# Loading queries as four tokens a partition and reading them with a stride on TensorE, with later state copies and score pairs

## The chip, the cores and the metric

One core of one Trainium2 chip. The metric is the device time of one execution in microseconds (us). Every time below is a median of several executions, but for three kernels that were run once; "the span" is the length of the one execution that the profiler recorded, some 1 to 2 us shorter. The granted TensorE clock of the kernel before, as a share of full speed, was above 0.99.

## The reference, cut to what matters

Linear attention with decay ("retention"), then a two-layer network with a tanh GELU, on B = 8 batches, H = 8 heads, S = 576 tokens, D = 64:

```python
scores = scale * np.matmul(q, k.transpose(0, 1, 3, 2))
gamma = 1.0 - 2.0 ** (-5.0 - np.arange(H))
Dmat = np.where(rel >= 0, gamma[:, None, None] ** rel, 0.0)      # rel = i - j
attn_out = np.matmul(scores * Dmat, v)
x = attn_out.transpose(0, 2, 1, 3).reshape(B * S, H * D)         # 4608 x 512
h = x @ w_in                                                     # 512 -> 2048
out = gelu_tanh(h) @ w_out                                       # 2048 -> 512
```

## The kernel before: the parts that matter

The 512 first tokens of a batch are four chunks c of 128 tokens, the other 64 are a tail. q and k are loaded as fp32, cast to fp16 with the decay folded in, and transposed, so that the head dimension lies on the partitions (tile `tt`: [128, q or k, 16 blocks, 128 tokens]). Per chunk, TensorE makes the scores `st` from k and q, VectorE masks them, and TensorE makes the values `xs` from them and v and adds what the state of all earlier chunks (`tbd`) gives for q. ScalarE copies `xs` as fp16 to `xT`, the input of the network. Its first layer gives `hp`, which ScalarE turns into `gT` with the gelu. The second layer is seven products of halves, summed in `opA`, `opB` and `opC`; for these VectorE makes sums `s` of parts of `gT` (the profile's lines call the sums `s` or `gT`). `ost` is a tile of the output. `cq` and `ck` are the casts of q and k, `eq` and `ek` those of the tail, `ld` and `lt` what was loaded. Batches 0 and 1 already load q with four consecutive tokens on a partition (1 KB runs); batches 2 to 7 load one token a partition (256 B runs):

```python
def load(b, key, c, u=0):
    ...
    elif key == "q" and b < NQ:                       # NQ = 2
        nc.sync.dma_start(
            out=t.rearrange("p (h x) -> p h x", h=2),
            in_=src[b, 2 * c : 2 * c + 2, 0:M0, :].rearrange("h (p j) d -> p h (j d)", j=QT),   # 1 KB runs
        )
    else:
        nc.sync.dma_start(
            out=t.rearrange("p (h d) -> p h d", d=D),
            in_=src[b, :, 128 * c : 128 * c + 128, :].rearrange("h s d -> s h d"),              # 256 B runs
        )
```

For batches 0 and 1 the permutation of the tokens is undone by the TensorE transposes, which write PSUM with a step of four (`turn_q4`). From batch 3 on the transpose is a DMA (`turn_dma`), which undoes nothing. The reads of q, by scores and by states:

```python
def tq(b, c, p):                                      # the moving operand: 128 tokens
    d, o = turned(b, c)
    return d[:, 1, 4 * p + c if b < NQ and c < NC else o + p, :]
...
# score(), two heads of a pair in the two row groups:
nc.tensor.matmul(st[hl][:, 128 * p : 128 * p + 128], d[r, 0, o + p, :], tq(b, c, p)[r], start=True, stop=True)
...
# inter(), "states" in this text:
nc.tensor.matmul(xs[:, 128 * p : 128 * p + 128], tbd[b % 2][:, c - 1, p, :], tq(b, c, p),
                 start=False, stop=True, skip_group_check=True)
...
# put(): ScalarE brings the values to the network's input
src = xs.rearrange("p (n g t) -> p g n t", n=HP, g=2)
nc.scalar.copy(out=xT[:, g0 : g0 + 2], in_=src)
```

The network of batch t runs interleaved with the attention of batch t + 1. A stage counts TensorE steps u of some 0.86 us, and attention work hangs on them:

```python
def states(t, u, b, c, tag):
    ...
    def sp(n, hl):                                    # ScalarE copies a state into tbd
        at(t, u + 2 + 2 * n + hl, lambda: spread(b, c + n, A.copy, (hl,)))
...
            u0, u1, u2, u3 = (8, 14, 19, 25) if t == 2 else (7, 13, 19, 25) if t == 3 else (6, 12, 19, 25)
            scores(t, u0, (b, 0, ...), (b, 1, ...), *tail)
        states(t, u1, b, 2, "t0")
        values(t, u1, (b, 0, "t1"), (b, 1, "t2"), ...)
        scores(t, u2, (b, 2, ("hp", "hp")), (b, 3, ("t1", "t2")))
```

## Time and profile before

| | before |
|---|---|
| time, median of the first 3 runs | 304.36 us (304.33 to 305.08) |
| span of the profiled execution | 302.8 us |
| busiest engines | TensorE 96%, VectorE 58%, ScalarE 57%, GpSimd 40% |
| fifth matmul of the network to the last matmul, from start to start | 277.1 us |
| last matmul's start to the end of the span | 4.76 us |

The last two rows are read from the trace's records of TensorE. The last but one is called the network stretch below; it begins with the fifth matmul, because the four before it wait in part for the last casts of the weights. Two more are needed here, the groups that the strided read will touch, with shapes kept apart. Columns: line, engine, operation, output<-input, shapes, count | busy us, mean ns of one | idle time before.

```profile
L317 PE MATMUL st<-tt 64*128 64x128 f16 x256 | 10.8, 218 | 1.2 <-DMA tt<-cq 0.5 <-ACT xT L405 0.5
L388 PE MATMUL xs<-tt,tbd 128*128 128x128 f16 x96 | 8.5, 221 | 0.0
```

The mean of 218 ns is not the cost of a matmul: successive matmuls overlap, and the recorded end is modelled. 256 scores are busy for 10.8 us together. The cost is the distance from start to start, which the chain of work that ended last gives in order of time (start, us, engine, what, line, count):

```profile
139.65 0.55 PE st L317 x16
...
146.38 0.55 PE xs L388 x8
```

Sixteen scores, two at a time, are eight steps; eight states are eight steps. From records start to start each is 56 ns, like the contiguous transposes of 128 columns in the same trace.

### The profile page before, as it was taken

How to read it: one execution, taken by the hardware profiler on the slowest of the kernel's cores; microseconds unless marked ns; L12 is line 12 of the kernel's file. 1: busy time of each engine (PE TensorE's matmuls, PEld its weight loads, DVE VectorE, ACT ScalarE, POOL GpSimd, SP SyncE). 2: the span in 40 equal slices, each digit the busy share in tenths (PEclk: the TensorE clock that was granted, in tenths of full speed). 3: DMA queues.
4: the chain of work that ended last, by engine and by line, in shares of the span. 5: the costliest groups of instructions: out<-in, count | busy, mean ns of one | idle time of the engine just before them, and what ended most of it. 6: DMA issues, size and time to landing. Idle time of an engine off the chain costs nothing.

```text
span 302.8 us, 6867 instructions
## 1 busy us (share of the span) xinstructions
PE 291.9 (96%) x2747; PEld 197.4 (65%) x2747; DVE 175.9 (58%) x359; ACT 173.0 (57%) x332; POOL 120.2 (40%) x178
## 2 busy tenths in 40 slices
PE   6899999999999999999999999999999999999994
PEld 2568755788784588458845884578456844784583
DVE  6650879678962866386547653855396435342423
ACT  6676417998657573658366736593647246316620
POOL 8668315550924179106910591049757110000000
PEclk9999999999999999999999999999999999999998
DMA  7999999999999996999599959953962140103004
GB/s 203 216 296 391 387 286 224 203 263 242 201 189 230 201 261 125 221 208 255 100 219 209 239 66 203 225 133 65 276 79 60 32 157 11 26 20 121 2 0 139
DMA packets 130592, 52.87 MB, mean 175 GB/s; under 512 B 118785, under 2 KB 121345, under 8 KB 130561
## 3 DMA queue, kind: packets, MB, share of 16 engines
q1 hardware_dynamic: 128544, 48.77, 74.2%
q0 software_dynamic: 1536, 3.15, 4.6%
q10 hardware_dynamic: 480, 0.52, 0.6%
q8 instruction: 21, 0.34, 0.5%
q14 instruction: 11, 0.08, 0.1%
HBM read 36.70 MB, written 9.44 MB: 152 GB/s over the span
## 4 chain that ended last, share of the span: by engine, by line
PE 74%; ACT 9%; DMA 5%; SPq 4%; POOL 3%; issue 2%; DVE 1%; POOLq 0%
PE hp L415 28%; PE opB L508 11%; PE opC L508 8%; PE hp L432 7%; PE opA L508 6%; PE op L451 4%; SPq L95 3%; DMA tt<-cq 3%; PE st L317 3%; PE xs L367 2%; ACT gT L421 2%; DMA ld<-in_moe_w_in_dram 2%; PE xs L388 2%; ACT xT L405 1%; PE us L338 1%
## 5 line engine op out<-in xcount | busy, mean ns | idle before, releaser
L415 PE MATMUL hp<-xT,w_in_sb 128*128 128x512 f16 x448 | 101.2, 379 | 0.3
L421 ACT ACTIVATE gT<-hp 128x512 f16<-128x512 f32 x112 | 66.9, 598 | 54.8 <-PE hp L415 46.6
L415 PEld LDWEIGHTS <-w_in_sb 128*128 128x128 f16 x448 | 42.9, 98 | 50.9 <-issue 3.2
L508 PEld LDWEIGHTS <-gT 128*128 128x128 f16 x512 | 49.9, 98 | 7.4
L324 DVE TENSOR_TENSOR ret<-st,cm 128x512 f16<-128x512 f32 x64 | 40.0, 683 | 8.4 <-PE st L317 8.4
L488 DVE TENSOR_TENSOR s<-gT 128x512 f16<-128x512 f16 x32 | 14.7, 458 | 50.0 <-ACT gT L421 49.0
L257 POOL TENSOR_TENSOR ck<-ld,sc 128x512 f16<-128x512 f32 x31 | 32.9, 1062 | 21.3 <-DMA ld<-in_k_dram 18.7
L508 PEld LDWEIGHTS <-s 128*128 128x128 f16 x384 | 36.5, 98 | 6.2 <-DVE s L489 1.6
L508 PE MATMUL opA<-w_out_sb,gT 128*128 128x256 f16 x256 | 30.6, 273 | 0.0
L508 PE MATMUL opB<-wt,gT 128*128 128x256 f16 x256 | 30.4, 273 | 0.0
L432 PE MATMUL hp<-xT,w_in_sb 128*128 128x256 f16 x256 | 29.8, 273 | 0.4 <-POOL w_in_sb L582 0.2
L432 PEld LDWEIGHTS <-w_in_sb 128*128 128x128 f16 x256 | 24.6, 98 | 3.7 <-POOL w_in_sb L582 0.5
L257 POOL TENSOR_TENSOR cq<-ld,sc 128x512 f16<-128x512 f32 x24 | 25.2, 1052 | 2.6 <-DMA ld<-in_q_dram 2.5
L751 POOL COPY gate<-s 128x1 f16<-128x1 f16 x5 | 0.9, 187 | 62.3 <-DVE s L491 62.3
L559 ACT COPY ost<-opA 128x512 f32<-128x512 f32 x8 | 4.7, 587 | 31.8 <-PE opA L508 31.8
L438 ACT ACTIVATE gT<-hp 128x512 f16<-128x512 f32 x32 | 19.0, 600 | 5.9 <-PE hp L432 5.8
L405 ACT CAST xT<-xs 128x512 f16<-128x512 f32 x32 | 18.5, 582 | 4.1 <-PE xs L388 3.8
L359 ACT CAST tbd<-ws 64x256 f16<-64x256 f32 x48 | 19.3, 402 | 1.3 <-DVE ws L354 0.5
L523 DVE TENSOR_TENSOR ost<-k,opC 128x512 f32<-128x512 f32 x15 | 10.3, 687 | 16.4 <-PE opC L508 16.1
L523 DVE TENSOR_TENSOR k<-k,opB 128x512 f32<-128x512 f32 (+1 forms) x18 | 11.3, 629 | 12.4 <-PE opB L508 10.5
L508 PE MATMUL opB<-wt,s 128*128 128x256 f16 x128 | 15.8, 273 | 0.8 <-DVE s L489 0.8
L244 ACT CAST cv<-ld 128x512 f16<-128x512 f32 x27 | 15.8, 616 | 0.3
(96 smaller groups left out, 368.1 us busy)
## 6 DMA issues: line engine op xcount, KB each, us to landing
ld<-in_q_dram SPq DMA_DIRECT2D x32, 256.0 KB, 5.2
ld<-in_k_dram SPq DMA_DIRECT2D x32, 256.0 KB, 5.2
ld<-in_v_dram SPq DMA_DIRECT2D x32, 256.0 KB, 5.1
out_dram<-ost SPq DMA_DIRECT2D x16, 512.0 KB, 5.2
ld<-in_moe_w_in_dram SPq DMA_DIRECT2D x16, 256.0 KB, 5.9
ld<-in_moe_w_out_dram SPq DMA_DIRECT2D x16, 256.0 KB, 5.4
lt<-in_k_dram POOLq DMA_DIRECT2D x16, 64.0 KB, 4.7
lt<-in_q_dram POOLq DMA_DIRECT2D x16, 64.0 KB, 4.5
```

What stands on the lines that cost most here:

```text
L244: eng.copy(out=dst, in_=raw)
L257: eng.tensor_tensor(out=dst.rearrange("p (h d) -> p h d", d=D), in0=raw.rearrange("p (h d) -> p h d", d=D), in1=sc[:, s0 : s0 + nh].unsque ...
L324: nc.vector.tensor_tensor(out=r, in0=st[hl][:, 0:w], in1=m.rearrange("p n i -> p (n i)"), op=ALU.mult)
L359: cp(out=(tbd[b % 2][r, c, :, r] if c < NC - 1 else tbt[b % 4][r, :, r]), in_=att[b]["w", c][r])
L405: nc.scalar.copy(out=xT[:, g0 : g0 + 2], in_=src)
L415: nc.tensor.matmul(hp.rearrange("p (g t) -> p g t", t=TL), w_in_sb[:, ct, 128 * fc : 128 * fc + 128], xT[:, o : o + TB // TL, ct, :], star ...
L421: nc.scalar.activation(out=gT[t][:, fc].rearrange("p i n -> p (i n)"), in_=hp, func=AF.Gelu_apprx_tanh)
L432: nc.tensor.matmul(hp[:, 256 * x : 256 * x + 256].rearrange("p (g t) -> p g t", t=TL), w_in_sb[:, ct, 128 * (f + x) : 128 * (f + x) + 128] ...
L438: nc.scalar.activation(out=gT[t][:, f : f + 2, 2 * u : 2 * u + 2, :].rearrange("p f i n -> p f (i n)"), in_=hp.rearrange("p (f n) -> p f n ...
L488: nc.vector.tensor_tensor(out=s["1"], in0=a21, in1=a22, op=ALU.add)
L508: nc.tensor.matmul(op[tag, u][:, HD * u : HD * u + HD], lhs(f), rhs[:, f], start=(new and (u == 0 or own) and f == 0), stop=(f == NH - 1), ...
L523: nc.vector.tensor_tensor(out=o, in0=a, in1=b, op=ALU.add)
```

## The change

The intent: fewer short DMA packets for q (1 KB runs instead of 256 B), no instruction more, since the permutation is undone where TensorE reads q; and a re-timing of ScalarE's state copies and of the score pairs, to take away the last waits of TensorE. The last two stores of a group of tokens become one. Core of the diff:

```diff
+    PQ = range(NQ, NPE)                      # NPE = 3: only batch 2 keeps the old load
...
-        elif key == "q" and b < NQ:
+        elif key == "q" and b not in PQ:     # load(), and the same line in cast()
...
     def tq(b, c, p):
         d, o = turned(b, c)
-        return d[:, 1, 4 * p + c if b < NQ and c < NC else o + p, :]
+        if b < NPE or c == NC:
+            return d[:, 1, 4 * p + c if b < NQ and c < NC else o + p, :]
+        return d[:, 1, 4 * p : 4 * p + 4, 32 * c : 32 * c + 32].rearrange("x j t -> x t j")
+
+    def like(b, c, x):                       # gives the output the same shape, still contiguous
+        return x if b < NPE or c == NC else x.rearrange("x (t j) -> x t j", j=QT)
...
-                end(keep["o1"][:, u], 1, u, slice(HD, DM))
+                if u:
+                    end(keep["o1"][:, u], 1, u, slice(HD, DM))
...
-                end(keep["o1"][:, u], 1, u, slice(0, HD))
+                end(keep["o1"][:, u], 1, u, slice(0, HD if u else DM))
...
-            at(t, u + 2 + 2 * n + hl, lambda: spread(b, c + n, A.copy, (hl,)))
+            at(t, u + wait + 2 * n + hl, lambda: spread(b, c + n, A.copy, (hl,)))
...
-            u0, u1, u2, u3 = 11, 17, 19, 25
+            u0, u1, u2, u3 = 11, 17, 20, 25
...
-            u0, u1, u2, u3 = (8, 14, 19, 25) if t == 2 else (7, 13, 19, 25) if t == 3 else (6, 12, 19, 25)
+            u0, u1, u2, u3 = (8, 14, 19, 25) if t == 2 else (7, 13, 19, 25)
...
-        states(t, u1, b, 2, "t0")
+        states(t, u1, b, 2, "t0", 6)
```

The moving operand of a strided read is 32 times 4 elements: the inner four stand in four blocks of 128 fp16, so 256 bytes apart, and each next group of four is one fp16 further on.

More of the change, by code (lines that the diff above doesn't have):

```diff
@@ L246, in cast @@
                 eng.tensor_copy(out=dst, in_=raw)
-        elif key == "q" and c < NC and b < NQ:
+        elif key == "q" and c < NC and b not in PQ:
             eng.tensor_tensor(
@@ L317, in score @@
                 nc.tensor.matmul(
-                    st[hl][:, 128 * p : 128 * p + 128], d[r, 0, o + p, :], tq(b, c, p)[r], start=True, stop=True
+                    like(b, c, st[hl][:, 128 * p : 128 * p + 128]), d[r, 0, o + p, :], tq(b, c, p)[r], start=True, stop=True
                 )
@@ L388, in inter @@
                 nc.tensor.matmul(
-                    xs[:, 128 * p : 128 * p + 128],
+                    like(b, c, xs[:, 128 * p : 128 * p + 128]),
                     tbd[b % 2][:, c - 1, p, :],
@@ L680, in scores, with states @@
         at(t, u, lambda: [score(*x) for x in xs])
-    def states(t, u, b, c, tag):
+    def states(t, u, b, c, tag, wait=2):
         def go():
```

## The prediction

The sum stays 304.36 - 2.5 - 0.4 = 301.5 us with a free read, and 308.9 us with one at half rate (+7.4).

> **What bounds the kernel now.** I read the page's part 1 and the slices first, then the group table, then who waited for whom, then the order in time around each TensorE wait, and the order in time of the last microseconds. Part 1 and the slices:
>
> ```profile
> span 302.8 us, 6867 instructions
> PE 291.9 (96%) x2747; PEld 197.4 (65%) x2747; DVE 175.9 (58%) x359; ACT 173.0 (57%) x332; POOL 120.2 (40%) x178
> ...
> PE   6899999999999999999999999999999999999994
> ...
> DMA  7999999999999996999599959953962140103004
> ```
>
> TensorE is busy in every slice but the first and the last, at full granted clock; the next engine is at 58%. Busy could still hide pacing by something else, so I looked at starts: 16 matmuls of 256 columns run 1.75 us on the chain of work that ended last (109 ns each), 24 of 512 columns 5.29 us (220 ns each). TensorE is streaming. So the time falls only by what TensorE loses in waits, at the head, or at the tail, and rises by whatever makes a matmul slower. The DMA row is full up to two thirds of the span, but loads run ahead of their use: they matter only where TensorE waits for them. Who waited for whom, PE only, 60 to 240 us, is the full list of such places:
>
> ```profile
> PE opB L508 <- DVE s L489: 0.8, 3, 0.5
> PE st L317 <- DMA tt<-cq: 0.5, 1, 0.5
> PE st L317 <- ACT xT L405: 0.5, 1, 0.5
> ```
>
> That list understates the loss, since a matmul's recorded end is modelled and overlaps the next start. The order in time on PE lets me measure from start to start:
>
> ```profile
> 78.32 0.45 PE L317 MATMUL st<-tt 64*128 64x128 f16 x9
> 79.27 0.38 PE L317 MATMUL st<-tt 64*128 64x128 f16 x7 [0.50 <-ACT xT L405]
> ...
> 181.05 6.43 PE L415 MATMUL hp<-xT,w_in_sb 128*128 128x512 f16 x28
> 187.99 0.62 PE L317 MATMUL st<-tt 64*128 64x128 f16 x16 [0.51 <-DMA tt<-cq]
> ...
> 230.35 0.82 PE L508 MATMUL opB<-wt,s 128*128 128x256 f16 x6
> 231.64 1.26 PE L508 MATMUL opB<-wt,s 128*128 128x256 f16 x10 [0.47 <-DVE s L489]
> ```
>
> First: 9 matmuls that run in pairs of row groups need about 0.28 us, and took 0.95: 0.66 lost. Second: 28 x 0.216 = 6.05, plus 0.31 for the last one and the change of tiling, puts the scores at 187.41; they began at 187.99: 0.58 lost. Third: 6 x 0.109 = 0.65 against 1.29: 0.64 lost; the same wait costs 0.33 near 168.2 and 0.33 near 199.6. Total 2.5 us.
>
> [...] the transposes of line 273 write with a step of four fp32, those of line 287 contiguously, both warm and with 128 columns:
>
> ```profile
> 46.14 0.60 PE L273 MATMUL tr<-ident,cq 128*128 128x128 f16 x4
> ...
> 55.92 0.39 PE L287 MATMUL tr<-ident,ck 128*128 128x128 f16 x4
> ```
>
> Taking off the last matmul's own 0.27 and 0.22 us, three steps take 0.33 and 0.17: 0.11 against 0.056 us each, half rate. No matmul here reads SBUF with such a step, so for the read itself this trace is silent. [...] The page counts 118785 of 130592 packets under 512 B; in the trace's packet records a 256 B packet takes 23 ns in the mean and a 1024 B one 53, so four short ones cost 93 against 53. [...]
>
> **The change, part by part.**
>
> *Query loads.* 20 tiles (5 batches x 4) go from 1024 packets of 256 B to 256 of 1024 B: 1024 x 23.2/16 = 1.49 us of the 16 engines each, to 256 x 52.7/16 = 0.84. That frees 13 us of DMA time between 60 and 210 us. Only the transpose that the scores at 188 us wait for touches the path. Its chain before is eight POOL casts of 1.0 us, then 9.3 us of transpose, not a load, so this part is worth 0 to 0.5 us and overlaps with the later scores below. The POOL cast of the new layout is the form of line 248, 1052 ns at its fastest on POOL against 1044 for the old: nothing.
>
> *Strided reads.* For batches 3 to 7 the moving operand becomes 32 tokens x 4, with an inner step of 128 fp16 (256 B)[...]. Per batch: 32 score matmuls, two at a time, are 16 steps; 12 state matmuls (line 388) are 12 more. 5 x 28 = 140 steps of 56 ns on the path. No instruction is added. If the read is free: 0. If it runs at half rate as the PSUM write does: 140 x 0.053 = +7.4 us. At quarter rate, +22.
>
> *State copies four units later, pairs one unit later.* Before the last gelu of a stage ScalarE does two 0.58 us copies (line 405), a tail cast (0.40) and a 0.40 us state copy; that delays the gelu, then DVE's s, then opB. In the instruction order of the changed kernel only one 0.58 us copy and the tail cast remain ahead of it. The third stage already has this placing, and shows no such wait. I take all 1.3 us off. Moving the scores one unit (0.86 us) later covers the 0.58 lost at 188. In the first stage scores move by 0.87 us and no state copies stand between the two xT copies: the 0.66 goes. Sum 2.5, no instruction added.
>
> *Tail.* The stores of one token group become one, so each queue issues 5 final stores, not 6. On DVE the last sum starts at 298.30 and takes 0.42, yet the last ScalarE-queue store is issued only at 299.71:
>
> ```profile
> 298.30 0.42 DVE L523 TENSOR_TENSOR ost<-k,opB 128x256 f32<-128x256 f32 x1 [0.45 <-PE opB L508]
> ...
> 298.48 0.58 ACTq L536 DMA_DIRECT2D out_dram<-ost  x1
> ...
> 299.71 0.47 ACTq L536 DMA_DIRECT2D out_dram<-ost  x1
> ```
>
> Just before it that queue holds a semaphore wait (299.66), on the semaphore that its second store of 296.25 used: with six stores it waits for an older one to land. With five it can issue near 298.8, as SyncE's did (298.84). Up to 0.9 us; since SyncE's last store and the bigger merged one must land too (1.9 to 3.4 us after issue), I take 0.4.
>
> Sum with a free read: 304.36 - 2.5 - 0.4 = 301.5. With a half-rate read: 308.9.
>
> **The rivals.**
>
> *A: the strided read halves the scores' and states' rate.* For: [...] the measured PSUM analogue. Against: the pattern is another memory; [...] and a design that puts a step on the busiest engine to help one that is not the bound makes sense only if its author had found it cheap. I give it 0.34. 308.9 us, 1.5% slower.
>
> *B: the read is free and the waits go.* For: the measured losses have exactly the placing that is changed, and the third stage is a control within this trace. 0.58. 301.5 us.
>
> *C: waits return elsewhere.* ScalarE's state copies now fall among value casts and the copies of A and B results; scores one unit later leave DVE less time before the values at unit 13. Slack for it: DVE is at 58%, and values follow six units (5 us) behind. It would give back 0.5 to 1.5 us: 302 to 303.
>
> *D: a quarter rate or worse,* or row-group pairs that no longer run side by side: 313 to 326. 0.05.
>
> **Range and chances.** The two main outcomes lie 7.4 us apart, and the profile before can't decide between them. The middle of my belief is inside the free branch with a little of C: 302.0. The range must span both: 300.5 (all waits and the whole tail won) to 309.5. More than 2% faster means under 298.3, some 3 us below everything that I can name: 0.02. More than 2% slower means over 310.5: rival D, and A with some of the gains lost: 0.12. Within 2%: 0.86.
>
> **What would show it.** Right: in the groups, line 317's and 388's successors keep about 216 to 219 ns; sixteen scores still stretch 0.62 us in the order in time; no PE wait on DVE s, on tt<-cq or on xT; packets down by about 15360; the last ScalarE-queue store within 0.3 us of DVE's last sum. Rival A: sixteen scores take over 0.9 us, eight line-388 matmuls over 0.9 instead of 0.62, and PE stays busy with 7 us more. Rival C: the PE waits list shows new pairs. I am wrong altogether if the scores keep their rate and the span still does not fall, or if a stretch outside 60 to 240 us and the tail moves by over 0.5 us.

## The result, and the profile after

The kernel after takes **325.15 us** (324.87 to 325.76, 4 runs) against 304.35 (304.2 to 305.08, 4 runs) for the kernel before on the same chip, and the result is correct. The ratio is 1.068, with a 95% interval of 1.066 to 1.071. A ratio here is the mean time of one kernel's fast runs over the mean of the other's of the same rounds, so it is not quite the ratio of the medians. Every experiment is compared in that way with runs of the kernel before on its own chip.

The page's first parts, after: span, busy time and instructions, the slices of TensorE and of the DMA engines, the packets.

```profile
span 323.1 us, 6865 instructions
PE 314.2 (97%) x2747; PEld 205.6 (64%) x2747; DVE 175.3 (54%) x359; ACT 173.4 (54%) x332; POOL 120.7 (37%) x178
...
PE   7899999999999999999999999999999999999994
...
DMA  7999999999999739970999089904960121103004
...
DMA packets 115071, 52.87 MB, mean 164 GB/s; under 512 B 98272, under 2 KB 105696, under 8 KB 115040
```

The same 2747 matmuls are busy for 22.3 us more (314.2 against 291.9), and TensorE's weight loads (PEld) for 8.2 us more, while no other engine's busy time moves by more than 0.6 us. The packets fell by 15521, as intended. Nothing in the slices shows the loss: the slower TensorE looks as busy here (97%) as the faster one (96%). The two groups, after:

```profile
L323 PE MATMUL st<-tt 64*128 64x128 f16 x256 | 23.6, 327 | 0.1
L394 PE MATMUL xs<-tt,tbd 128*128 128x128 f16 x96 | 18.1, 329 | 0.0
```

These groups also hold the 96 scores and 36 states of batches 0 to 2, which are unchanged, so the means of 327 and 329 understate the strided ones. The two groups' busy time grew by 12.8 and 9.6 us, and their idle time shrank: 22.4 us, all of TensorE's growth. One stage in the chain of work that ended last:

```profile
145.52 1.85 PE st L323 x16
...
153.53 1.85 PE xs L394 x8
```

0.55 us became 1.85 for the same sixteen scores and eight states. Start to start, in the trace's records, one step takes 218 to 220 ns instead of 56. Who waited for whom, TensorE only, from 60 to 265 us, is now a single line:

```profile
PE opB L514 <- DVE s L495: 0.4, 1, 0.4
```

So the waits that the change aimed at are nearly all gone, and the kernel is 20.8 us slower. At the end of the program (order in time) the last sum of VectorE and the last stores are these:

```profile
318.66 1.52 ACTq L542 DMA_DIRECT2D out_dram<-ost  x2
...
318.95 0.42 DVE L529 TENSOR_TENSOR ost<-k,opB 128x256 f32<-128x256 f32 x1 [0.45 <-PE opB L514]
```

In the records, ScalarE's last store is issued at 319.59, 0.22 us after the sum ends; before it was 0.98 us after. From the last matmul's start to the end the span takes 4.49 us instead of 4.76.

### The profile page after: what moved, and what is told of

Its sections match the earlier page's. It is cut to its first block, busy times and chain, and to the rows that moved or that the text cites. A ratio compares the mean times of both kernels' runs of the same rounds, so it can differ in the third digit from the quotient of the medians.

```text
span 323.1 us, 6865 instructions
## 1 busy us (share of the span) xinstructions
PE 314.2 (97%) x2747; PEld 205.6 (64%) x2747; DVE 175.3 (54%) x359; ACT 173.4 (54%) x332; POOL 120.7 (37%) x178
## 4 chain that ended last, share of the span: by engine, by line
PE 89%; SPq 4%; ACT 3%; DMA 2%; DVE 1%; issue 1%; POOL 0%; ACTq 0%
PE hp L421 30%; PE opB L514 13%; PE opC L514 9%; PE opA L514 8%; PE hp L438 7%; PE st L323 7%; PE xs L394 5%; PE op L457 4%; SPq L96 3%; PE xs L373 2%; DMA ld<-in_moe_w_in_dram 2%; PE us L344 2%; PE tr L288 1%; ACT gT L444 1%; SPq L90 1%
## 5 line engine op out<-in xcount | busy, mean ns | idle before, releaser
L249 POOL TENSOR_TENSOR cq<-ld,sc 128x512 f16<-128x512 f32 x22 | 24.3, 1108 | 0.1
L323 PE MATMUL st<-tt 64*128 64x128 f16 x256 | 23.6, 327 | 0.1
L323 PEld LDWEIGHTS <-tt 64*128 64x128 f16 x256 | 10.8, 103 | 12.8 <-issue 3.8
```

The costliest lines, as they stand in the source:

```text
L249: eng.tensor_tensor(out=dst.rearrange("p (j l d) -> p l j d", j=QT, l=2), in0=raw.rearrange("p (l j d) -> p l j d", l=2, j=QT), in1=sc[:, ...
L323: nc.tensor.matmul(like(b, c, st[hl][:, 128 * p : 128 * p + 128]), d[r, 0, o + p, :], tq(b, c, p)[r], start=True, stop=True)
```

## The experiments

The theory after the result: the strided read of the moving operand alone makes the kernel slow, and 140 steps of +0.164 us (220 less 56 ns) are 22.9 us. Rivals: the later pairs or state copies opened something; the new loads did; only a step that is a power of two, as 256 bytes is, is slow; pairs of row groups no longer run side by side.

### The change without its stride, and the stride without the rest

```diff
# e1_retune_only, against after
-    PQ = range(NQ, NPE)
+    PQ = range(NQ, B)
-        if b < NPE or c == NC:                 # tq(); like() accordingly
+        if True:
```

> The changed kernel with its later schedule and merged store, but queries of batches 3 to 7 loaded in 256 B pieces and read contiguously as before; correct. Theory (the strided read alone makes it slow: 140 matmul steps, each 220 ns instead of 56, so 140 x 0.164 = 22.9 us): 325.15 - 22.9 = 302.2 us, between 301.7 and 302.8. Rival 1 (part of the loss is the schedule, e.g. state copies that now stand in the way on ScalarE): above 304. Rival 2 (part of the loss is the new loads or the POOL cast, which waits would show): above 302.8 only if the stride costs less than 22.9.

Measured: 302.67 us (302.37 to 303.29) beside 304.71, ratio 0.994 (0.9925 to 0.9957).

`e2_stride_only` is the kernel before with only the edits of `load`, `cast`, `tq` and `like` shown above:

> The kernel before with nothing but the new query loads and the strided reads; schedule and stores as before; correct. Theory: 304.35 + 22.9 = 327.2 us, or up to 1 us less, since the slower scores give the transposes and ScalarE more time and so hide some of the 2.5 us of old waits: 326 to 327.5. If the schedule were what slows the change: about 304 to 310.

Measured: 327.04 us (326.98 to 327.61), ratio 1.074 (1.0725 to 1.0762), with the groups of the after kernel:

```profile
L323 PE MATMUL st<-tt 64*128 64x128 f16 x256 | 23.8, 327 | 0.7 <-ACT xT L411 0.5
L394 PE MATMUL xs<-tt,tbd 128*128 128x128 f16 x96 | 18.1, 329 | 0.0
```

The whole loss belongs to the loads and the strided reads. The re-timing wins 2.0 us without them (`e1`), and with them 1.9 us (`e2` against after, by their ratios to the kernel before, since they ran on different chips). The network stretch takes 277.1 us before, 275.0 in `e1` without the stride, and 297.6 after: 22.6 us for the loads and the stride, against 22.9 from 140 steps. In the chain of work of `e1` scores and states are back:

```profile
139.38 0.55 PE st L323 x16
...
146.10 0.55 PE xs L394 x8
```

### Scores strided, states not

```diff
# e11_scores_strided, against after; wrong on purpose: states read contiguous, other tokens
-                    like(b, c, xs[:, 128 * p : 128 * p + 128]),
+                    xs[:, 128 * p : 128 * p + 128],
                     tbd[b % 2][:, c - 1, p, :],
-                    tq(b, c, p),
+                    turned(b, c)[0][:, 1, 4 * p + c, :],
```

> The changed kernel with the strided read in the scores alone; the states (the products with the running state) read the right number of queries contiguously, which are the wrong tokens, so the result is wrong on purpose. Theory: 5 x 16 steps x 0.164 = 13.1 us over e1, 315.8 us; the states' 60 steps were the other 9.8. Rival (scores in pairs of row groups hide part of it): under 313.

Measured: 315.96 us in one look (beside a median of 305.06 for the kernel before on this chip). In the chain of work that ended last the scores stay slow, the states are back:

```profile
143.66 1.84 PE st L323 x16
...
151.67 0.55 PE xs L394 x8
```

The time alone is one look, so the sum is taken from the traces. The network stretch of `e11` is 288.9 us, 13.9 more than that of `e1`. Of this 0.95 us is a wait that the edit itself made: it also changed which blocks the states of batch 2 read, and one of them waits at 77.26 us for ScalarE's copy of a transpose. The other 12.9 us belong to the 80 steps of scores (13.1 worked out). The after kernel's stretch is 8.7 us longer than that of `e11`, which still contains this wait, so the 60 steps of states cost 9.7 us (9.8 worked out). The loss adds up by steps, and both kinds of step lose 0.16 us each.

### The read by itself

Two small kernels run only 16 matmuls of 128 columns for each form, and then a few copies on ScalarE. Their outputs are wrong, which doesn't matter for the times. In the second, 14 dense matmuls of 512 columns precede each group, since in the first the granted clock was 0.50 in some groups (28.3 to 40.6 us and 48.1 to 53.5 us). Each set of 14 between two groups took 3.02 to 3.07 us from start to start, 216 to 219 ns a matmul as in the full kernels at full clock, but for one of 4.48 us that starts at 76.03. Four of its forms:

```python
# e12_steps_warm, extract; e4_steps_alone is the same with other forms and without the dense ones between
for _ in range(16): matmul(t[:, 0:128], ident, src[:, 0:128])                                             # step 1
for _ in range(16): matmul(t[:, 0:128], ident, src[:, 0:512].rearrange('p (t s) -> p t s', s=4)[:, :, 0]) # step 4
for _ in range(16): matmul(t[:, 0:128]..., ident, blk[:, 0:32, 0:4])                          # runs of 4, 256 B apart
for _ in range(16): matmul(t[:, 0:128]..., ident, blk[:, 0:4, 0:32].rearrange('p j t -> p t j'))   # the change's read
```

In the two expectations the mechanism assumed is cut, since no run shows it.

> No attention and wrong output on purpose: groups of 16 matmuls of 128 columns, fp16, warm, one group a line, that differ in the moving operand's pattern alone. The number is the start-to-start time. Theory [...]: step 1 56 ns; step 8 and more (16 B and up) 218 ns; steps 2 to 5 between[...]; runs of 8 and more elements 256 B apart near 56; the change's 32 x 4 218, with rows of 264 B as well. Rival (power-of-two conflict of 256 B steps): rows of 264 B near 56, and steps 3 and 5 fast. Rival (any second dimension costs): runs of 32 slow. Side by side: PSUM writes with a step of 4 fp32 109 ns; two row groups with the 32 x 4 read still overlap (one step of 218 ns for two); a stationary operand with a step of 128 B unknown, 56 if its load hides. ScalarE copies with a permuted read or write: 0.58 us contiguous, unknown otherwise.

> As e4_steps_alone (wrong output on purpose), with 14 dense matmuls ahead of each group so that the clock stays full, since in e4 it was granted at half for some groups. Theory [...]: step 1 and 2 56 to 58 ns, step 4 116, step 6 170, step 8 and 16 218 to 230, runs of 2 110, runs of 4 56. Open: 64 x 2, which took 123 at half clock[...]. 16 x 8 and 8 x 16 as 32 x 4: 218. Inner step of 64 B: 218. PSUM writes with a step of 2 or 32 fp32: 109. ScalarE writing SBUF with a step of 4, 8, 16 B: 0.59 for contiguous, 1.28 for 8 B and, [...] 0.59 for 4 B and 1.3 or more for 16 B; reading PSUM with a step of 512 B 0.59.

The order in time on TensorE in the second one, cut to the groups with step 1, 4 and 8, runs of four elements, and the read of the change, with the dense matmuls (line 47) that follow each:

```profile
20.45 1.06 PE L60 MATMUL m<-src,ident 128*128 128x128 f16 x16
21.34 3.19 PE L47 MATMUL m<-src,ident 128*128 128x512 f16 x14
...
28.31 2.02 PE L66 MATMUL m<-src,ident 128*128 128x128 f16 x16
30.15 3.20 PE L47 MATMUL m<-src,ident 128*128 128x512 f16 x14
...
38.95 3.79 PE L72 MATMUL m<-src,ident 128*128 128x128 f16 x16
42.56 3.20 PE L47 MATMUL m<-src,ident 128*128 128x512 f16 x14
...
57.14 1.06 PE L81 MATMUL m<-src,ident 128*128 128x128 f16 x16
...
66.05 3.67 PE L87 MATMUL m<-src,ident 128*128 128x128 f16 x16
69.54 3.20 PE L47 MATMUL m<-src,ident 128*128 128x512 f16 x14
```

Read from the start of a group to the start of the next: step 1 takes 0.89 us for 16, or 56 ns each; step 4 (line 66) 1.84 us, 115 ns; step 8 (line 72) 3.61 us, 226 ns; the change's read (line 87) 3.49 us, 218 ns; runs of four (line 81) take 0.91 us, 57 ns. The table, in ns per matmul of 128 columns, is from the records of both kernels, where the usual distance is a little above these means. "Blocks" counts, from the addresses, how often the read goes on to another block of 16 bytes, to sort the times by.

| moving operand | blocks | ns |
|---|---|---|
| contiguous | 16 | 56 |
| step 2 fp16 | 32 | 58 |
| step 3 | 48 | 88 |
| step 4 | 64 | 116 |
| step 6 | 96 | 171 |
| step 8 | 128 | 227 |
| step 16 | 128 | 232 |
| runs of 2, 256 B apart | 64 | 112 |
| runs of 4, 256 B apart | 32 | 57 |
| 32 x 4, inner step 256 B (the change) | 128 | 218 to 220 |
| 32 x 4, inner step 264 B (granted clock 0.51) | 128 | 220 |
| 32 x 4, inner step 64 B | 128 | 217 |
| 64 x 2, inner step 256 B | 128 | 123 |
| PSUM written with step 2 or 32 fp32 | | 109 |

The time grows with the step up to 8 fp16, or 16 bytes (227 ns), and hardly beyond (232 ns for a step of 16); hence the size of the blocks. All reads but one fit 1.7 to 1.8 ns per block, or 56 ns where that is more. This is a fit to the table; what lies behind it the traces do not show. The rival that only a power of two is slow is excluded: a step of 3 took 88 ns and one of 6 took 171, inner steps of 264 and of 64 bytes took 220 and 217 ns like that of 256, and runs of four elements 256 bytes apart took 57. So is the loss of pairs: two row groups with the change's read still started 3 ns apart in the first small kernel, and a pair then took 220. The first kernel ran partly at half clock (0.5 granted in some groups); there the PSUM write with a step took 213 ns, twice its 109, and runs of four 107 instead of 57, but step 16 took 232 at both clocks and 64 x 2 took 123 at both. So the time of those two reads did not follow the granted clock. The row of 64 x 2 stays open: its 128 blocks took 123 ns, where 32 x 4 with as many took 218 to 220. The first kernel also read the stationary operand with a step of 64 fp16: 94 ns a matmul in the mean instead of 56. The change has no such read.

ScalarE's copies of 512 elements a partition from PSUM to fp16 in SBUF took 586 ns contiguous, and 728, 1291 and 2420 ns when they wrote SBUF with steps of 4, 8 and 16 bytes. Reading PSUM with a step of 128 bytes (first kernel) or 512 bytes (second) took 586 ns; one copy, right behind the strided writes, took 922.

### The same loads, read in runs

The 1 KB loads do not force a stride on TensorE. Within a chunk the four blocks hold 32 tokens each; read in the order block, token, the read has four runs of 32 fp16. Scores and values then come out in that order, a permuted causal mask `cmj` is needed, and the copy from `xs` to `xT`, which exists anyway, has to put the tokens back. The masks became fp16 to make room; VectorE's masking took 681 ns with them and 682 before.

```diff
# e3_runs_of_32, against after
-        return d[:, 1, 4 * p : 4 * p + 4, 32 * c : 32 * c + 32].rearrange("x j t -> x t j")
+        return d[:, 1, 4 * p : 4 * p + 4, 32 * c : 32 * c + 32]
-        m = cm if c < NC else tm
+        m = (cm if b < NPE else cmj) if c < NC else tm
+        if b >= NPE:                                     # put(): ScalarE writes xT with a step of 4 fp16
+            nc.scalar.copy(
+                out=xT[:, g0 : g0 + 2].rearrange("p g n (t j) -> p g n j t", j=QT),
+                in_=xs.rearrange("p (n j g t) -> p g n j t", n=HP, j=QT, g=2),
```

> The changed kernel with the same 1 KB loads and the same query elements read, but in the order in which they lie: four runs of 32 tokens (64 B each) instead of 32 x 4 with a step of 256 B. The causal mask is permuted to that order (masks kept as fp16 for room), and the copy into xT, written with a step of 4 elements, puts the tokens back; correct. Theory (what costs is the inner step, not the loads and not a pattern of two dimensions): scores and states back to 56 to 60 ns a step, 302 to 303 us, plus at most 1 us if the 20 copies with a step are slower. Rival (any pattern that jumps by 256 B within a matmul is slow): well above 310 us.

Measured: 305.07 us (305.0 to 307.63), correct, ratio 1.004 (1.0007 to 1.007). TensorE's groups were back at 56 ns a step, but my expectation missed by more than it allowed. Group and waits of TensorE (60 to 240 us):

```profile
L416 ACT CAST xT<-xs 128x512 f16<-128x512 f32 x20 | 25.5, 1303 | 2.6 <-PE xs L398 2.6
```

```profile
PE opB L524 <- DVE s L505: 2.2, 4, 1.1
```

The 20 copies take 1303 ns instead of 586. ScalarE is not the bound, but these copies stand ahead of the last gelu of a stage, which VectorE's sums and then TensorE wait for: 2.2 us in four places. (This trace is of the slowest of the four runs, 307.63 us; the others took 305.0 to 305.1. Set beside the trace of `e5` below, it has already lost 2.4 us by 64 us, before any of these copies, and it loses 2.4 more at the four places.) So the step was put on the read of PSUM, with the write to `xT` contiguous:

```diff
# e5_runs_psum_step, against e3
-                out=xT[:, g0 : g0 + 2].rearrange("p g n (t j) -> p g n j t", j=QT),
-                in_=xs.rearrange("p (n j g t) -> p g n j t", n=HP, j=QT, g=2),
+                out=xT[:, g0 : g0 + 2].rearrange("p g n (t j) -> p g n t j", j=QT),
+                in_=xs.rearrange("p (n j g t) -> p g n t j", n=HP, j=QT, g=2),
```

> As e3_runs_of_32, correct, but the copy that puts the tokens back writes xT contiguously and reads PSUM with the step of 32 fp32 (128 B). In e4 that form took ScalarE 586 ns a copy against 1281 for the write with a step of 8 B. Theory (e3's 2.4 us over e1 are those 20 copies, 1303 ns against 586, delaying the gelus and DVE's s): the copies are back at 0.59 us and the time at e1's 302.7 us, within 0.6; the 1 KB loads then gain nothing further, being off the path. Rival (the 1 KB loads or the fp16 masks cost something, or the jump by 256 B does): 304 to 305 stays.

Measured: 302.61 us (302.49 to 303.18) beside 304.56, correct, ratio 0.994 (0.9926 to 0.9955). The same 20 copies:

```profile
L416 ACT CAST xT<-xs 128x512 f16<-128x512 f32 x20 | 11.4, 583 | 2.6 <-PE xs L398 2.6
```

TensorE's two groups in this run, to compare with those of the kernel before and after:

```profile
L327 PE MATMUL st<-tt 64*128 64x128 f16 x256 | 10.6, 218 | 0.1
L398 PE MATMUL xs<-tt,tbd 128*128 128x128 f16 x96 | 8.5, 221 | 0.0
```

So the loads of the change cost nothing in this form, and no gain of theirs is resolved: with the old loads and the same re-timing the ratio was 0.9941 on another chip, here 0.9940. The freed DMA time lay beside the path. Per DMA engine, packets took 238 to 242 us in the six traces of whole kernels with the old loads, and 225 to 233 in the six with the new; the prediction had 13 us less.

### The parts of the re-timing

`e9_pairs_only` is the kernel before with only the two lines of `u0, u1, u2, u3` of the change; `e10_state_copies_only` has only the `wait` argument and its 6; `e7_tail_only` only the merged last store.

> The kernel before with the later pairs alone (scores and values of stages 4 to 6, and the second scores of stage 1, one unit later); state copies and stores as before; correct. Theory: with the values at unit 13 the state copies start at unit 15, after the last gelu, so this part alone takes away the waits for tt<-cq (0.58), for xT (0.66) and two of the three for DVE s (0.33 each): about 1.9 us, 302.6 us, and the later state copies of the change add nothing. Rival (the prediction's reading, that the state copies are what holds the gelu up): the DVE s waits stay, only 1.2 us gained.

Measured: 303.39 us (302.64 to 303.7) beside 305.06, ratio 0.994 (0.9918 to 0.9965). TensorE's waits in the trace from 60 to 240 us:

```profile
PE opB L508 <- DVE s L489: 0.4, 1, 0.4
```

> The kernel before with the later state copies alone; correct. Theory: one 0.40 us copy less ahead of the last gelu of stages 4 to 6 removes the two 0.33 us waits; the transposes are still waited for (0.58) and about half of the xT wait goes: 1.0 us gained, 303.5 us. Rival (only the pairs matter): nothing, 304.5.

Measured: 304.4 us (303.71 to 305.08), ratio 0.998 (0.9958 to 1.0009), so the time does not resolve it. The waits do:

```profile
PE opB L508 <- DVE s L489: 0.5, 1, 0.5
PE st L317 <- ACT xT L405: 0.2, 1, 0.2
PE st L317 <- DMA tt<-cq: 0.2, 1, 0.2
```

The later pairs alone take away four of the five waits: that for `xT`, that for the DMA transpose, and two of the three for VectorE's s. The later state copies alone take away those two for s as well, and only part of the others. Either suffices for those two. The network stretch says the same: 275.0 us with the pairs alone, as in `e1`, and 275.9 with the state copies alone, against 277.1 before. With the later pairs in place, no gain of the state copies is shown.

> The kernel before with the merged final store alone; correct. In the changed kernel the time from the last matmul's start to the end of the span fell from 4.76 to 4.49 us: theory 304.4 - 0.3 = 304.1 us, a ratio of 0.999, at the edge of what five rounds resolve; the last ScalarE-queue store starts within 0.3 us of DVE's last sum instead of 1.0 after it. Prediction's figure 0.4; if nothing, 1.000.

Measured: 304.42 us (303.99 to 305.85), ratio 1.0004 (0.9983 to 1.0025). The trace has 4.59 us from the last matmul's start to the end, against 4.76. A gain of 0.2 us is below what five rounds resolve: not shown in the time.

### The wait that stayed

In `e1_retune_only` one wait for s remains, near 230 us, 0.52 us long measured from start to start. In order of time:

```profile
228.46 0.73 DVE L494 TENSOR_TENSOR s<-gT 128x512 f16<-128x512 f16 x1 [1.53 <-ACT gT L427]
...
228.97 0.69 POOL L258 TENSOR_TENSOR ek<-lt,sc 128x256 f16<-128x256 f32 x1
229.22 0.72 DVE L495 TENSOR_TENSOR s<-s,gT 128x512 f16<-128x512 f16 x1
229.62 0.78 POOL L258 TENSOR_TENSOR eq<-lt,sc 128x256 f16<-128x256 f32 x1
229.87 0.83 DVE L496 TENSOR_TENSOR gT<-gT 128x512 f16<-128x512 f16 x1
```

VectorE's sums take 0.72 to 0.83 us where, away from such casts, they take 0.42: GpSimd casts a tail at the same time. `e6_gate_only` lets the two casts wait for VectorE's fourth sum, to see whether they are what makes the sums long (only the overlap and the times are measured):

```diff
# e6_gate_only, against e1
+        if b == 5:
+            at(*k, lambda: nc.gpsimd.tensor_copy(out=gate, in_=gs[6]["4"][:, NH - 1, 1, 0:1]))
         at(*k, lambda b=b: (new_tail(b), [cc(b, key, NC, P) for key in "kq"]))
```

> e1_retune_only with one 1-element POOL copy that holds POOL's two tail casts of batch 5 back until DVE's last s of stage 6 is done; correct. Theory: the one wait of PE for DVE s that the change left (0.52 us near 229 us) is not ScalarE's doing [...]: the wait goes, 302.67 - 0.5 = 302.2 us. Rival (ScalarE's order still delays it): no change, 302.6 to 302.8.

Measured: 302.32 us (301.79 to 302.9), ratio 0.993 (0.9914 to 0.9949); against `e1`'s 0.9941 on another chip that is not resolved. In order of time, the first two sums:

```profile
228.50 0.42 DVE L494 TENSOR_TENSOR s<-gT 128x512 f16<-128x512 f16 x1 [2.11 <-ACT gT L427]
...
228.96 0.42 DVE L495 TENSOR_TENSOR s<-s,gT 128x512 f16<-128x512 f16 x1
```

The sums are back at 0.42, the wait is gone, and the network stretch takes 274.6 instead of 275.0 us. The gate also moved GpSimd's DMA issues that stood around the casts, and the first slow sum overlaps more of an issue than of a cast. But in the trace of `e1` the 13 sums that overlap such issues and no cast took 0.41 to 0.43 us. So GpSimd's casts caused this wait; ScalarE did not.

### A version that beats both

`e8_all_runs_gate` takes the runs of `e5` and the gate of `e6`, and reads batches 0 and 1 in runs too, so that their transposes write PSUM contiguously (`t[:, 128 * j : 128 * j + 128]` in `turn_q4`), at full rate instead of half (in its trace a group of four takes 0.39 us, in that of `e5` 0.60):

> A version that may beat both kernels, correct: e5_runs_psum_step with the same reading for batches 0 and 1 too, whose 32 query transposes then write PSUM contiguously (56 instead of 109 ns warm), and the gate of e6_gate_only. Theory: batch 1 gains 16 x 0.053 = 0.85 us, batch 0 up to 0.5 at the head where loads set the pace, the gate 0.5: e5 less 1.3 to 1.8, about 301.2 us. If e5 stays slow, that much slower.

Measured: 302.12 us (301.2 to 302.43), correct, ratio 0.992 (0.99 to 0.9933), the lowest median of all, though not resolved from `e6` on the same chip. The expectation missed by 0.9 us. The cheaper transposes brought TensorE to a place where it waits for VectorE's mask of the scores of batch 1:

```profile
49.56 0.38 PE L292 MATMUL tr<-ident,ck 128*128 128x128 f16 x4 [0.47 <-DVE ret L334]
```

Start to start this wait costs 0.63 us, of the 0.85 us that the expectation had worked out for these 16 transposes; the rest of the miss is not accounted for.

## Why the prediction was wrong, point by point

- **What bounds the kernel.** Right. TensorE streams, and what slowed the matmuls here showed in full: 22.6 us more in the network stretch, for 22.9 worked out from the steps. In the trace before, matmuls of 128, 256 and 512 columns mostly start 56, 109 and 216 ns apart, so the reading held.
- **The count of strided steps, 140, and where they lie.** Right, shown by `e11`: 80 and 60 of them, additive.
- **The cost of a strided step: the step that failed.** The prediction gave 0.58 to a free read and 0.34 to half rate (+0.053 us a step), and only 0.05 to its rival D of quarter rate or worse. Measured: 218 to 220 instead of 56 ns, +0.164 us a step, so "At quarter rate, +22" was the case. Two reasons had led away from it; a third rested on an assumed mechanism. *The PSUM analogue* of 109 ns was taken as the size of the penalty; it belongs to another memory, where the times came out otherwise (109 ns for steps of 2 and of 32 fp32 alike, while the read of SBUF took 58, 116 and 227 ns for steps of 2, 4 and 8 fp16). *"Its author had found it cheap"* is no evidence on hardware at all. The other half of rival D, that the pairs of row groups no longer run side by side, did not happen: in the stage of the after trace shown above, too, the two scores of a pair start 3 or 4 ns apart.
- **Query loads, 0 to 0.5 us.** Right at its lower end: packets down 15521 (predicted about 15360), and `e5` shows no gain over the old loads. The new GpSimd cast has a mean of 1108 ns (the prediction took its fastest, 1052), and no wait of TensorE in the after trace leads to it from 60 us on.
- **State copies and pairs, -2.5 us.** Nearly the right size: 2.1 us in the trace of `e1`. The attribution was partly wrong. The pairs alone give all of what is shown; the third wait for s had GpSimd's casts as its cause, was not removed, and kept 0.52 of its 0.64 us.
- **Tail, -0.4 us.** The mechanism was right: the last ScalarE store is issued 0.22 instead of 0.98 us after the sum. The size was too big. Counted from the last matmul's start, the last store lands 0.39 us sooner in the trace of after, but the span ends only 0.27 us sooner; the time alone does not resolve even that.
- **The sum.** The prediction's 301.5 had a free read. With the measured terms the sum is 304.36 - 2.1 - 0.3 + 22.9 = 324.9, against 325.15 measured. Rival D's range of 313 to 326 holds it.
- **Range and chances.** The range ended at half rate, because two main outcomes were taken from an analogue. "Slower" got 0.12. An unmeasured rate on the busiest engine should have spread the range to quarter rate.
- **The marks.** The listed test for rival A (sixteen scores over 0.9 us) was met with 1.85. The PE waits list came out as predicted but for one, and with no new pair in it, so rival C did not happen either. It shows that a clean list of waits says nothing about the time of the work itself.

## What to carry to other kernels

When TensorE is the bound, let it read its fp16 moving operand in runs of four or more, or with a step of at most two: runs of four and a step of two took 57 and 58 ns per 128 columns here at full clock, beside 56 for a contiguous read, while runs of two took 112, a step of four 116 and a step of eight 227. A permutation that has to be undone belongs to an instruction that already exists and that read PSUM with a step at no cost here, ScalarE's copy of the values (583 ns against 585 without the step), not to the matmul's read and not to an SBUF write (1303 ns). And before a stride goes onto the busiest engine, time 16 such matmuls by themselves: a loss inside busy time appears in no list of waits.
